# Filler matmuls in more of TensorE's early waits, 256 columns wide instead of 128

## The chip, the cores and the metric

One core of a Trainium2 chip runs the whole kernel. The metric is device time in microseconds, from the start of the program to its end, as the median of the runs of this kernel; the profile shows one execution more closely. The core has a matrix engine (TensorE, PE), a vector engine (VectorE, DVE), an engine for elementwise functions (ScalarE, ACT), a general one (GpSimd, POOL) and queues that issue transfers (among them SyncE, SP). Each works through its own list of instructions in order and waits at semaphores for the others.

## What is computed

A linear attention over 4 batches x 4 heads x 1088 tokens x 32, and behind it a layer with 2048 hidden units. Both are cut here to what matters.

```python
phi(x): a = x @ S1.T; b = x @ S2.T; outer product of a and b per token, 64 values
q_p, k_p = phi(q), phi(k)
kv = einsum('bhsf,bhsd->bhfd', k_p, v);  z = sum(k_p, axis=2)
attn = (q_p @ kv) / (q_p @ z + 1e-6)         # to x: 4352 tokens x 128
h = x @ w_in                                 # 4352 x 2048
out = (h - tanh(h)) @ w_out                  # 4352 x 128
```

## The kernel before

All work is described as operations with a list of what each reads and writes and a cost in nanoseconds. A planner, `_Prog.schedule` (line 139), walks through them once while the program is built. For each engine it keeps the time at which the engine is free, takes the operation that can start first (with keys for ties and for a window of similar starts), and appends it to that engine's list. Costs are written with the operations: `_v(n)` for VectorE, `_a(n)` for ScalarE, `_pe(ns)` for TensorE, and the landing times of the first loads are given by hand. The lists that come out are what the chip runs; waits at semaphores are added by `sync` (line 263). So a planned time decides only the order and, as follows, the fillers.

A filler is a matmul of zeros (tile `zz`, line 434) into a PSUM bank that nothing uses yet, `pso`. When the planner places an operation on TensorE, it looks at the planned wait ahead of it (line 203). If the wait is longer than a limit, `fill` (line 244) puts as many fillers into it as fit. The limit is 60 ns while TensorE becomes free before 7600 ns of the plan (`SOLID`), and `WIDE_GAP` = 1000 ns after. Fillers stop for good when the planner gives out the first bank for output products (`filler[2].used`), which is at o0.0 (line 996). The planned cost of one is 54 ns, doubled while the plan is before 13000 ns (`COLD`). Before `SOLID` a filler may end up to 100 ns after the wait's planned end (`OVER`); after it, it must end 60 ns ahead.

The order of the work in the head, with its lines: the k of batch 0 is transposed on VectorE (L636) and multiplied with the sketches on TensorE (L647, in two parts), brought back by VectorE (L652), and a Gram product of it is taken (L692, two parts), whose small result goes through ScalarE (L698) and one more product (L702). Then the first part of the q sketch (L666, 4 products), then kv (L760, 72 products of v and k's outer products, which VectorE makes at L730). ScalarE copies the result (L373), TensorE transposes it (L777), and the rest of the q sketch follows (L666, 14 products), which ScalarE copies out for VectorE (L678). Then comes the attention's numerator (L866), which gives x, then the layer: h (L981), tanh on ScalarE (L986), and the output products (L996, L1000), which VectorE transposes (L1005) and SyncE writes out. Between these TensorE also transposes w_in (L940) and multiplies it with w_out (L952). ScalarE casts w_in (L934) and copies its transposes (L945). Batches 1 to 3 of the attention follow interleaved with the layer, which runs over groups of 192 to 512 columns (`GCOLS`) and 16 blocks of hidden units each.

Loads are issued at L474 from the queues of SyncE, ScalarE and GpSimd, some of them held until earlier ones have landed.

Of the kernel before, what the change touches and what calls it, by code (L numbers as in the profile page):

```python
# [13 lines left out]
BF16 = mybir.dt.bfloat16  # L14
# [75 lines left out]
class _Prog:  # L90
# [2 lines left out]
    SOLID = 7600.0  # L93
    WARM = 7900.0
    COLD = 13000.0
    WIDE_GAP = 1000.0

    def __init__(self):
        self.ops = []
# [39 lines left out]
    def schedule(self, filler=None):  # L139
# [30 lines left out]
        while n < len(self.ops):  # L170
# [31 lines left out]
            if e == "tensor":  # L202
                if filler is not None and t - free[e] > (60.0 if free[e] < self.SOLID else self.WIDE_GAP) and not filler[2].used:
                    t = max(t, self.fill(filler, free[e], t))
# [39 lines left out]
    def fill(self, filler, a, b):  # L244
        t = a
        while True:
            cold = 2.0 if t < self.COLD else 1.0
            occ = 54.0 * cold
            if t + occ + (60.0 if t > self.SOLID else -self.OVER) > b:
                break  # L250
            o = _Op()
            o.engs = {"tensor": (occ, 215.0)}
            o.fn, o.key, o.dma, o.name, o.mode = filler[0], 0, 0, "fill", "128x128"
            o.deps, o.users, o.vals = {filler[1]: True}, [], []
            o.filler = True
            o.eng, o.t0, o.t1, o.lat = "tensor", t, t + occ, 215.0
            o.inc, o.sem, o.waits, o.known = False, None, [], {}
            o.seq = len(self.order["tensor"])
            self.order["tensor"].append(o)
            t = o.t1  # L260
        return t
# [58 lines left out]
def _v(n):  # L320
    return {"vector": (n / 0.96 + 64.0, 143.0)}
# [22 lines left out]
def bass_polysketch_attn__then__act_tanh_shrink_kernel(  # L344
# [10 lines left out]
    P = _Prog()  # L355
    uid = [0]

    def sb(name, shape, dtype=FP32):
        uid[0] += 1
        return nc.alloc_sbuf_tensor(f"{name}_{uid[0]}", shape, dtype).ap()  # L360

    def ps(name, n=1):
        uid[0] += 1
        return nc.alloc_psum_tensor(f"{name}_{uid[0]}", [128, n * 512], FP32).ap()

    def sbv(name, shape, dtype=FP32):
        return _Val(ap=sb(name, shape, dtype))
# [7 lines left out]
    def slices(pl, parts):  # L375
# [6 lines left out]
    bank_o = _Pool([ps("pso"), psa[:, 1024:1536]], True)  # L382
# [48 lines left out]
    wiT = [sbv("wiT", [128, 8, 128], BF16) for _ in range(2)]  # L431
    wch = sbv("wch", [128, DM], BF16)
    wcl = sbv("wcl", [128, DM], BF16)
    zz = sbv("zz", [128, 256], BF16)

    zop = P.add(_v(128), lambda e, n: e.memset(zz.ap[:, :], 0.0), w=[zz], key=-99000)  # L436
    filler = (lambda e, n: e.matmul(bank_o.slots[0][0][:, 0:128], zz.ap[:, 0:128], zz.ap[:, 128:256],  # L437
                                    start=True, stop=True), zop, bank_o)

    def pool_op(fn, r=(), w=(), n=100, key=-50000.0):  # L440
        return P.add(_g(n), fn, r=r, w=w, key=key)
# [4 lines left out]
        fill=1.0, base=0, channel_multiplier=1), r=[ident], w=[ident])  # L446
# [10 lines left out]
    for pl, f, val in ((kT_p, lambda a: a[:, 1088:1152], 0.0),   # L457
                       (m_p, lambda a: a[:, :, 8:9], 1e-6)):
        for i, s_ in enumerate(pl.slots):
            o = pool_op(lambda e, n, a=f(s_[0]), val=val: e.memset(a, val), n=64, key=-49000)  # L460
# [83 lines left out]
    t = T_FIRST  # L544
# [478 lines left out]
    for name in ORDER.split():  # L1023
        b = int(name[1])
# [85 lines left out]
```

## Time and profile before

| what | us |
|---|---|
| median of 5 runs (lowest, highest) | 109.80 (109.14, 110.00) |
| the profiled execution's own time | 109.84 |
| its span, from the first to the last instruction | 107.8 |
| busy: PE, ACT, DVE, POOL | 99.7, 83.4, 67.2, 5.0 |
| fillers (L437): 48 products, busy | 5.0 |
| mean granted TensorE clock | 0.968 of full |

The fillers run in three groups, 36 from 1.06 us, 8 from 5.77 and 4 from 6.71. The program has 3434 recorded instructions, of which 1462 are matmuls and as many weight loads.

How to read it: times of the timeline are counted from the first instruction. The page gives the busy share of each engine in 40 slices of 2.7 us, in tenths (9 is 90% or more), and the granted TensorE clock in tenths of full speed. A matmul's duration includes the time that its last column takes to leave the array, which overlaps with the next matmul, so counts times durations are not sums. In a list of stretches the columns are start and end, length, and for each engine its busy time and number of instructions, then the granted clock, the share of the DMA engines and GB/s. In a timeline they are start, duration, engine, line, operation, what it writes and reads, and in brackets the engine's idle time before it and what ended that. A chain is followed back from the last instruction to whatever released it at each step.

### The profile page before, as it was taken

What the parts mean: (1) busy time and instruction counts of PE and PEld (TensorE: products, weight loads), DVE (VectorE), ACT (ScalarE), POOL (GpSimd) and SP (SyncE); (2) the same over time, 40 slices, a digit from 0 to 9 for tenths busy, and PEclk for the clock granted to TensorE, in tenths of its full rate; (3) what the DMA queues carried; (4) which work ended last, traced back from release to release, by engine and by line L of the source; (5) the groups of instructions that cost most, each with busy time, mean ns of one, the idle gap of its engine ahead of it and who ended that gap; (6) DMA issues with size and microseconds to landing.
All of it is one profiled execution on the core that took longest, in us unless ns stands there. A gap on an engine that the chain in (4) does not pass through costs nothing.

```text
span 107.8 us, 3434 instructions
## 1 busy us (share of the span) xinstructions
PE 99.7 (92%) x1462; PEld 53.3 (49%) x1462; DVE 67.2 (62%) x114; ACT 83.4 (77%) x174; POOL 5.0 (5%) x23
## 2 busy tenths in 40 slices
PE   6974899899999999999999999999999999999960
PEld 6834788475664446543346443444433443344730
DVE  4679834998992999999999990899620020020210
ACT  0400368999648888878898987999989999999950
POOL 5600420000000000000000000000000000000000
PEclk9996559999999999999999999999999999999999
DMA  2999899776039736006930150033003315004153
GB/s 65 227 247 218 245 125 271 269 186 207 14 41 277 204 88 138 6 6 124 275 106 0 20 84 0 6 50 47 0 0 45 59 19 78 0 15 68 17 76 58
DMA packets 26431, 10.73 MB, mean 100 GB/s; under 512 B 21153, under 2 KB 24241, under 8 KB 26417
## 3 DMA queue, kind: packets, MB, share of 16 engines
q1 hardware_dynamic: 22368, 8.69, 35.0%
q0 software_dynamic: 2112, 0.54, 5.1%
q10 hardware_dynamic: 1936, 1.29, 5.0%
q8 instruction: 11, 0.18, 0.7%
q14 instruction: 4, 0.02, 0.1%
HBM read 8.81 MB, written 2.23 MB: 102 GB/s over the span
## 4 chain that ended last, share of the span: by engine, by line
PE 40%; ACT 32%; DVE 13%; DMA 9%; issue 2%; SPq 1%; DVEq 0%
ACT th L986 27%; PE pso L996 11%; PE psh L981 9%; DMA vL<-in_v_dram 7%; PE psa L866 6%; PE psa L760 3%; DMA sq<-in_S_dram 3%; ACT xT L373 3%; DVE w L730 2%; DVE abc L807 2%; DVE qp L850 2%; DVE ot L1005 1%; PE pso L1000 1%; PE psh L666 1%; PE psa L799 1%
## 5 line engine op out<-in xcount | busy, mean ns | idle before, releaser
L986 ACT ACTIVATE th<-psh 128x512 bf16<-128x512 f32 (+4 forms) x114 | 63.3, 656 | 3.0 <-PE psh L981 2.8
L981 PE MATMUL psh<-xT,wi 128*128 128x512 bf16 (+4 forms) x142 | 44.0, 348 | 0.4 <-ACT th L986 0.4
L996 PE MATMUL pso<-th,wo 128*128 128x512 bf16 (+3 forms) x128 | 40.4, 358 | 0.3 <-DVE ot L1005 0.2
L996 PEld LDWEIGHTS pso<-th,wo 128*128 128x128 bf16 x128 | 11.7, 97 | 16.4 <-ACT th L986 4.5
L981 PEld LDWEIGHTS psh<-xT,wi 128*128 128x128 bf16 x142 | 13.4, 98 | 12.1 <-ACT th L986 1.6
L1005 DVE STREAM_TRANSPOSE ot<-pso 128x512 f32<-128x512 f32 (+3 forms) x8 | 5.2, 645 | 15.7 <-PE pso L996 15.7
L855 DVE STREAM_TRANSPOSE qpT<-qp 128x768 f32<-128x768 f32 (+1 forms) x14 | 12.1, 861 | 0.4
L730 DVE TENSOR_TENSOR w<-abk 128x768 f32<-128x768 f32 (+2 forms) x12 | 11.0, 943 | 0.1
L850 DVE TENSOR_TENSOR qp<-ap,abc 128x768 f32<-128x768 f32 (+1 forms) x13 | 10.7, 826 | 0.1
L986 ACT ACTIVATE th<-psa 128x1024 bf16<-128x1024 f32 (+2 forms) x10 | 8.6, 907 | 0.0
L866 PE MATMUL psa<-qpT,kvb 32*32 32x128 f32 (+4 forms) x336 | 8.2, 309 | 0.1
L866 PE MATMUL psh<-qpT,kvb 32*32 32x128 f32 (+4 forms) x112 | 8.2, 310 | 0.0
L996 PE MATMUL psa<-th,wo 128*128 128x512 bf16 (+1 forms) x32 | 7.4, 314 | 0.3 <-ACT th L986 0.2
L866 PEld LDWEIGHTS psa<-qpT,kvb 32*32 32x32 f32 x336 | 5.0, 103 | 3.1 <-DVE qpT L855 1.2
L1005 DVE STREAM_TRANSPOSE ot<-psa 128x512 f32<-128x512 f32 (+1 forms) x2 | 1.1, 550 | 8.6 <-PE psa L996 8.6
L437 PE MATMUL pso<-zz 128*128 128x128 bf16 x48 | 5.0, 290 | 1.1 <-DVE zz L436 1.1
L610 DVE STREAM_TRANSPOSE qT<-qL 128x576 f32<-128x576 f32 (+3 forms) x8 | 5.4, 708 | 0.4 <-DMA qL<-in_q_dram 0.4
L981 PE MATMUL psa<-xT,wi 128*128 128x512 bf16 (+1 forms) x18 | 5.6, 349 | 0.0
L437 PEld LDWEIGHTS pso<-zz 128*128 128x128 bf16 x48 | 4.4, 137 | 1.5 <-DVE zz L436 1.1
L804 DVE STREAM_TRANSPOSE abc<-psh 128x288 f32<-128x288 f32 x3 | 1.4, 483 | 5.1 <-PE psh L799 5.0
L698 ACT ACT_TABLE_LOAD x1 | 1.3, 1283 | 4.2 <-issue 4.2
L373 ACT CAST xT<-psa 128x64 bf16<-128x64 f32 (+4 forms) x11 | 4.4, 457 | 0.0
(87 smaller groups left out, 99.5 us busy)
## 6 DMA issues: line engine op xcount, KB each, us to landing
vL<-in_v_dram SPq DMA_DIRECT2D x11, 144.0 KB, 3.8
wif<-in_moe_w_in_dram SPq DMA_DIRECT2D x4, 256.0 KB, 6.3
out_dram<-ot SPq DMA_DIRECT2D x16, 64.0 KB, 2.0
kL<-in_k_dram SPq DMA_DIRECT2D x3, 288.0 KB, 3.1
qL<-in_q_dram SPq DMA_DIRECT2D x3, 288.0 KB, 3.3
kL<-in_k_dram SPq DMA_DIRECT2D x3, 256.0 KB, 3.0
qL<-in_q_dram SPq DMA_DIRECT2D x3, 256.0 KB, 3.9
wo<-in_moe_w_out_dram POOLq DMA_DIRECT2D x2, 256.0 KB, 5.9
```

What stands on the lines that cost most here:

```text
L373: return e.copy(o, i) if name == "scalar" else e.tensor_copy(o, i)
L437: filler = (lambda e, n: e.matmul(bank_o.slots[0][0][:, 0:128], zz.ap[:, 0:128], zz.ap[:, 128:256], start=True, stop=True), zop, bank_o)
L610: P.add(_v((z - a) * 32), lambda e, n: e.transpose(qTs[b][:, a * 32:z * 32], val.ap), r=[val], w=tvs, key=nk(), name=f"qT{b}.{i}")
L730: P.add(_v(nx * 64), lambda e, n: e.tensor_tensor(out=wv.ap[:, 0:nx * 64].rearrange("p (x i j) -> p x i j", i=8, j=8), in0=abh(0)[:, :, :, ...
L760: i = e.matmul(bk[2].ap[h * 32:(h + 1) * 32, 0:64], vL[b][:, h, blk * 32:(blk + 1) * 32], wvs[b, p].ap[:, (bi * 4 + h) * 64:(bi * 4 + h + ...
L850: P.add(_v(cn * 256), lambda e, n, qp=qp, c0=c0, cn=cn: e.tensor_tensor(out=qp.ap[:, 0:cn * 256].rearrange("p (x i j) -> p x i j", i=8, j= ...
L855: P.add(_v(cn * 256), lambda e, n, qp=qp, o0=o0, cn=cn: e.transpose(qt.ap[:, o0 * 256:(o0 + cn) * 256], qp.ap[:, 0:cn * 256]), r=[qp], w=[ ...
L866: i = e.matmul(banks[g].ap[h * 32:(h + 1) * 32, 0:nb * 32], kvb.ap[g * 32:(g + 1) * 32, x, h * 32:(h + 1) * 32], qq[g * 32:(g + 1) * 32, 0 ...
L981: return e.matmul(hv.bank(j // per)[:, c:c + n_], wib[:, jb * 128:(jb + 1) * 128], xt, start=True, stop=True)
L986: return e.activation(out=th.ap[:, 0:m * n_].rearrange("p (j x) -> p j x", x=n_), in_=i, func=AF.Tanh, scale=-1.0)
L996: fn = lambda e, n, x=x, st=st, sp_=sp_: e.matmul(ov.ap[:, 0:n_], wob[:, x, :], ths[x][0].ap[:, ths[x][1]:ths[x][1] + n_], start=st, stop=sp_)
L1005: P.add(_vp(n_), lambda e, n: e.transpose(ot.ap[:, 0:n_], ov.ap[:, 0:n_]), r=[ov], w=[ot], key=-60000, name=f"ot{gi}")
```

## The change

The limit for waits that begin after 7600 ns falls from 1000 to 150 ns. `fill` tries a filler of 256 columns first and takes one of 128 when the wide one does not fit; a wide one may not end after the wait's planned end, even before `SOLID`. The tile of zeros grows by 128 columns, with the planned cost of its memset.

```diff
-    WIDE_GAP = 1000.0
+    WIDE_GAP = 150.0
...
             cold = 2.0 if t < self.COLD else 1.0
-            occ = 54.0 * cold
-            if t + occ + (60.0 if t > self.SOLID else -self.OVER) > b:
-                break
+            margin = 60.0 if t > self.SOLID else -self.OVER
+            w = 1
+            occ = 107.0 * cold
+            if t + occ + max(margin, 0.0) > b:
+                w = 0
+                occ = 54.0 * cold
+                if t + occ + margin > b:
+                    break
             o = _Op()
             o.engs = {"tensor": (occ, 215.0)}
-            o.fn, o.key, o.dma, o.name, o.mode = filler[0], 0, 0, "fill", "128x128"
+            o.fn, o.key, o.dma, o.name, o.mode = filler[0][w], 0, 0, "fill", "128x128"
...
-    zz = sbv("zz", [128, 256], BF16)
-
-    zop = P.add(_v(128), lambda e, n: e.memset(zz.ap[:, :], 0.0), w=[zz], key=-99000)
-    filler = (lambda e, n: e.matmul(bank_o.slots[0][0][:, 0:128], zz.ap[:, 0:128], zz.ap[:, 128:256],
-                                    start=True, stop=True), zop, bank_o)
+    zz = sbv("zz", [128, 384], BF16)
+
+    zop = P.add(_v(192), lambda e, n: e.memset(zz.ap[:, :], 0.0), w=[zz], key=-99000)
+    filler = ([lambda e, n, w=w: e.matmul(bank_o.slots[0][0][:, 0:w], zz.ap[:, 0:128], zz.ap[:, 128:128 + w],
+                                          start=True, stop=True) for w in (128, 256)], zop, bank_o)
```

## The prediction

> **What bounds the kernel now.** I read the page's slices first, to see whether TensorE's clock ever falls.
>
> ```profile
> PE   6974899899999999999999999999999999999960
> ACT  0400368999648888878898987999989999999950
> PEclk9996559999999999999999999999999999999999
> ```
>
> A slice is 2.7 us. From 20 us to the end TensorE and ScalarE are both nearly full and the clock is whole, so that stretch will move only as a block. The one irregular place is the head: slices 5 to 7 (10.8 to 18.9 us) have a clock of 0.5 to 0.6. Second view: stretches of 3.41 us, laid so that they begin and end where the granted clock changes.
>
> ```profile
> core 0: us, PE busy (x), PEclk, DMA share, GB/s
> 5.71:9.12 3.41, 2.07 (x54) 1.00 0.99 233
> 9.12:12.53 3.41, 2.23 (x41) 0.50 0.97 238
> 12.53:15.95 3.42, 3.42 (x68) 0.50 0.97 153
> 15.95:19.36 3.41, 3.33 (x90) 1.00 1.44 287
> 101.27:104.68 3.41, 2.85 (x28) 1.00 0.31 45
> ```
>
> The clock is full up to 9.12, half from 9.12 to 15.95, full again after: 6.83 us, two of these stretches. Each follows the one before it: busy 2.07 of 3.41 (61%) and then half clock; 65% and still half; 100% and then full; 98% and 84% and still full. (The first fillers too ran slowly: 36 in 4.02 us, one every 0.107 us; those after 5.7 us 0.056 apart.) Third view: TensorE's timeline, with the waits in the brackets.
>
> ```profile
> 7.24 0.51 PE L647 MATMUL psh<-kT,wab 64*32 64x160 f32 x16
> 8.84 0.31 PE L692 MATMUL psa<-abk 128*32 128x32 f32 x10 [1.09 <-DVE abk L652]
> 9.42 0.29 PE L702 MATMUL psa<-gm,s2r 128*32 128x8 f32 x8 [0.28 <-ACT gm L698]
> 10.10 1.17 PE L666 MATMUL psa<-wq,qT 128*128 128x96 f32 x4 [0.38 <-DVE wq L715]
> 11.79 2.15 PE L760 MATMUL psa<-w,vL 128*32 128x64 f32 x72 [0.52 <-DMA vL<-in_v_dram]
> ...
> 19.64 0.39 PE L981 MATMUL psh<-xT,wi 128*128 128x256 bf16 x2 [0.36 <-ACT th L986]
> ```
>
> Last view: the chain that ended last, in order of time.
>
> ```profile
> 4.40 7.35 DMA vL<-in_v_dram
> 11.79 2.15 PE psa L760 x72
> 13.94 0.54 PE psh L940 x4
> 14.48 0.64 PE psa L777 x2
> 15.12 1.33 PE psh L666 x8
> 16.48 0.48 ACT abc L678
> ```
>
> Up to 11.75 us the end hangs on v's landing. Nothing that TensorE does earlier matters, and the half clock before 11.79 is free. From 11.79 to 16.48 the chain lies on TensorE at half clock: that is the price to be won or not.
>
> **The change, step by step.** Sum against the profiled execution: 109.84 us, of which 107.82 is span and 2.02 lies around it; the median of the runs shown is 109.80, so I take it as the same.
>
> *Where fillers go.* The limit WIDE_GAP applies to planned waits that begin after 7600 ns of the plan. The plan follows from the costs in the code; before, it has waits there of 858 ns (ahead of the second gram product), 467 (ahead of L702), 507 (ahead of the first L666), 118, 201 (ahead of L777) and 542 (ahead of h0.4, the 19.64 row). All are under 1000, so none was filled; five are over 150. A wide filler is planned at 214 ns (107 after 13000), a narrow one at 108 (54), with a margin of 60. So: 858 takes 3 wide and 1 narrow, 467 takes 1 and 1, 507 takes 2, 201 takes one narrow, 542 takes 4 and 1. In all 10 wide and 4 narrow.
>
> *The early fillers.* Of 48 narrow ones (36, 8, 4), the same arithmetic makes 18 wide and 1 narrow, 3 and 2, 1 and 2: 27 instructions and 49 units of 128 columns in place of 48. Records: 41 instead of 48, each with its weight load. The columns are the same, so the clock should still rise at 5.71. The first wait ends one unit later than before: the fillers ended at about 4.87, the next work started at 5.16, so 0.11 fits. The plan behind it moves by some 70 ns; the matmul order could then differ in a place, which I can't exclude and cost at nothing.
>
> *The larger memset.* VectorE's 0.17 us for 128 words becomes about 0.25; its next memsets end at 2.2 and it idles 0.52 until 2.72. Hidden, save that fillers start 0.07 later.
>
> *What the fillers cost in place.* TensorE runs in order, so the instruction behind a filler waits for it. A wide one counts as two units (the 256-wide L981 at 18.56 are 0.109 apart, four in 0.61). In the 1.09 wait: at 0.056 a unit, 7 units are 0.39, at half clock 0.75: room either way. Ahead of L702: 3 units, 0.17 or 0.32, against 0.28 shown (the product before is issued by about 8.95, its end holds a drain of 0.2): 0 to 0.05 late. Ahead of L666: 4 units, 0.22 or 0.43, against 0.38 and a similar drain: 0 to 0.1. Both lie before v's landing, which leaves 0.52. Ahead of L777: one unit, 0.06 or 0.11, beside ScalarE's copy (14.01 to 14.38) which L777 waits for: 0 to 0.1. Ahead of h0.4: 9 units at full clock, 0.50, against 0.36 plus the drain: 0 to 0.15; behind it ScalarE's tanh is queued after a copy at 19.96, so h0.4 has some 0.4 to spare. No row shows a change between filler and 32-column products with a wait this short; 0 to 0.1 each. I take 0.2 in all, ends 0 and 0.5.
>
> *What they do to the clock.* This is the whole question, and no row shows it; I bound it. Fillers raise the busy share of 5.71 to 9.12: the 1.09 wait gets 0.39 of streaming and about 0.17 of drain, 0.56; with the 0.28 wait's beginning 2.65 of 3.41, 78%. 61% let the clock fall, 84% kept it: 78 is nearer the upper. If it falls nevertheless, 9.12 to 12.53 gets both waits, 2.23 + 0.28 + 0.38 = 2.89, 85%: 65% did not raise it, 100% did, so it stands in the middle. If it stays, the same stretch runs at full clock and needs less time: 2.4 to 2.5 busy, about 72%, so it might fall at 12.53 instead.
>
> *A rule against it.* The Trainium skill (TensorE: Matmul & The Clock Gate, "Why this matters for your kernels") says that only pauses beyond about 3 us between bursts bring the half clock back. The row: the longest pause here is 1.09 us and the clock fell. By the rule waits of 0.3 to 1.1 us never mattered and the fillers give 0; by the row a thinly used stretch is enough, and filling is worth up to 1.3. The measurement decides. The same page (Part 1) has a window of 3.41 us that runs free of the kernel's start, which agrees with the 6.83 us here. If so, each execution has its own boundaries, and the median mixes the cases below.
>
> *What a full clock is worth.* With it from 11.79: the 72 products take 1.19 instead of 2.15 (the same 72 of a later batch, L745 at 41.84): 0.96. The two L777 products take 0.48 from start to next work, half of that gone: 0.24. Five of the first eight L666 products at 0.11 instead of 0.21: 0.45 (their starts before and after 15.95). TensorE: 1.65. ScalarE between 14.01 and 18.99 idles only 0.82, but it starts 0.96 earlier, so it follows: about 1.5 at the first tanh. The weights do not stop it: the first half of wo lands at 16.9, used at 19.87. If the clock returns only at 12.53, 28 of the 72 stay slow: 0.57 + 0.24 + 0.45, about 1.2. Less the 0.2 of fillers: 1.3 and 1.0. From there to the end work is in order and full, k and q of the next batch have landed before VectorE takes them, so the shift should reach the end. What is late next is ScalarE's own row of copies and tanh.
>
> **The rivals.**
> 1. Clock falls at 9.12, back at 12.53: 109.84 - 1.0 = 108.8. Chance 0.27.
> 2. Clock never falls: 109.84 - 1.3 = 108.5. Chance 0.26. For both: 78% and 85% against the rows.
> 3. Clock holds at 9.12, falls at 12.53, returns at 15.95: 52 of the 72 run fast (-0.65), L777 stays slow, and of the L666 products eight instead of five do (+0.3): -0.35, 109.5. Chance 0.15. For it: fillers are sized for half clock and cover only half a wait at full clock.
> 4. Not what it says: the fillers (zeros, 14 of them) don't tip any stretch, cost 0 to 0.2: 109.9. Chance 0.15.
> 5. Slower: the half clock is not removed but moved behind v's landing. In the old place 2.67 of its 6.83 us (9.12 to 11.79) cost nothing. If it begins at 12.53 and lasts two stretches, to 19.36, then all 14 L666 products are slow (nine more at +0.10, 0.9), and so are L866 and the transposes and first h products from 17.04 to 19.28 (2.2 us at full clock; half beside ScalarE, so 1.1 of it counts). Against the 0.65 won on the products: 0.9 + 1.1 - 0.65 = +1.35, about 111.2. It decides when 12.53 to 15.95 is not busy enough to raise the clock: it was 100%, and with fast products in front a wait for v's copy opens in it. Chance 0.17.
>
> **How the numbers follow.** The likeliest is case 1, 108.8. The range runs from 108.3 (case 2 and 0.2 less filler cost) to 110.2 (case 4 with its cost); outside lie case 5 and a tail. A measurement can tell about 0.5% (0.55 us) from no change. Faster by more: cases 1 and 2 and a third of 3: 0.58. Within: the rest of 3, and 4: 0.25. Slower: 0.17. Own range of the faster cases: 108.3 to 109.2.
>
> **What would show it.** L437 x41, 32 wide and 9 narrow; fillers in the waits ahead of L692, L702, L666, L777 and the third pair of L981. Granted clock of 9.12 to 12.53 and of 12.53 to 15.95: 1.00 in case 2, 0.50 and 1.00 in case 1. L760's 72 at 1.2 to 1.6 instead of 2.15; the copy L678 at 15.0 to 15.3 instead of 16.48; the first tanh near 17.7 instead of 18.99. I am wrong if the clock rows are as before, if v lands later, or if the head is earlier and the tanh after 20 us is not.

## The result and the profile after

| | before | after |
|---|---|---|
| median, us (executions) | 109.76 (79) | 108.74 (44) |
| the profiled execution: own time, span | 109.84, 107.8 | 108.84, 106.7 |
| mean granted clock of it | 0.968 | 0.996 |

The ratio is 0.9964, 95% interval 0.9945 to 0.9982: faster by 0.4%, where 0.9% was forecast. The median lies at the forecast 108.8. The two disagree because every ratio here leaves out each execution more than 1.5% above its own kernel's fastest among those timed together, which keeps 23 of 79 before (median 109.07) and 34 of 44 after (108.60). A ratio of this size is also near what one program against itself gave (0.9965, at the end of the experiments), so it alone doesn't show a gain; the medians and the granted clock do. Which groups of executions lie behind the two medians is the main finding below.

First the page's clock row of after, to hold against that of before, and the row of the fillers (count, busy time, mean ns).

```profile
PE   5997899899999999999999999999999999999960
PEclk9999999999999999999999999999999999999998
...
L442 PE MATMUL pso<-zz 128*128 128x256 bf16 (+1 forms) x41 | 7.9, 352 | 1.1 <-DVE zz L441 1.1
```

The hole in the clock is gone. Next, stretches of 3.41 us that begin where the clock first changed in this execution (6.97), with busy time, clock and DMA as before.

```profile
core 0: us, PE busy (x), PEclk, DMA share, GB/s
6.97:10.39 3.42, 2.50 (x53) 1.00 1.07 250
10.39:13.80 3.41, 2.94 (x88) 1.00 0.80 251
13.80:17.21 3.41, 3.36 (x93) 1.00 1.26 187
```

Here a stretch that was busy for 73% was followed by full clock; before, one of 61% was followed by half. The share alone does not decide it, as the repeats below show. Then TensorE's timeline.

```profile
5.79 1.44 PE L442 MATMUL pso<-zz 128*128 128x256 bf16 x7
7.45 0.51 PE L652 MATMUL psh<-kT,wab 64*32 64x160 f32 x16 [0.21 <-DVE kT L641]
7.88 0.27 PE L697 MATMUL psa<-abk 128*32 128x32 f32 x8
8.09 0.61 PE L442 MATMUL pso<-zz 128*128 128x256 bf16 x4
9.40 0.31 PE L697 MATMUL psa<-abk 128*32 128x32 f32 x10 [0.70 <-DVE abk L657]
...
10.66 0.69 PE L671 MATMUL psa<-wq,qT 128*128 128x96 f32 x4
11.73 1.21 PE L765 MATMUL psa<-w,vL 128*32 128x64 f32 x72 [0.38 <-DMA vL<-in_v_dram]
12.89 0.40 PE L945 MATMUL psh<-identb,wi 128*128 128x128 bf16 x4
13.12 0.27 PE L442 MATMUL pso<-zz 128*128 128x256 bf16 x1
13.44 0.44 PE L782 MATMUL psa<-ident,kvd 128*128 128x128 f32 x2
13.71 1.70 PE L671 MATMUL psh<-wq,qT 128*128 128x96 f32 x14
```

(Lines past 245 have moved by five.) The 72 products take 1.21 instead of 2.15, and the last L671 group starts 1.20 earlier, although the work in front of v's landing is later: the second Gram product (L697) at 9.40 instead of 8.84. The planner has put the second L652 ahead of the first L697. v hides that.

ScalarE's timeline shows how far the gain reaches. Before, then after: the first tanh and a later group of three.

```profile
18.99 1.08 ACT L986 ACTIVATE th<-psh 128x512 bf16<-128x512 f32 x2
...
25.63 1.39 ACT L986 ACTIVATE th<-psh 128x384 bf16<-128x384 f32 x3
```

```profile
17.29 1.08 ACT L991 ACTIVATE th<-psh 128x512 bf16<-128x512 f32 x2
...
24.56 1.33 ACT L991 ACTIVATE th<-psh 128x384 bf16<-128x384 f32 x3
```

1.70 us earlier at the first, 1.07 at the second, 1.07 at the end (span 107.8 to 106.7). So 0.6 us of the head's gain is lost between 17 and 25 us. It shows in the second of these lines of TensorE's timeline of after, inside the second run of numerator products:

```profile
20.61 0.24 PE L871 MATMUL psa<-qpT,kvb 32*32 32x96 f32 x1
21.28 0.27 PE L871 MATMUL psa<-qpT,kvb 32*32 32x96 f32 x2 [0.42 <-issue]
```

"issue" means that it waited for nothing that the profile shows. From the product before (20.61) to this one (21.28) 0.67 us pass. ScalarE then waits for the result, the copy to x. Its copy in after, and in the kernel `full_rate` below, which has the same order here, the same first tanh (17.28) and no such pause:

```profile
21.68 0.24 ACT L378 CAST xT<-psh 128x96 bf16<-128x96 f32 x1 [0.38 <-PE psh L871]
```

```profile
21.10 0.34 ACT L378 CAST xT<-psh 128x96 bf16<-128x96 f32 x1
```

So the pause costs 0.58, nearly all of the 0.6. (This numerator starts only 1.37 earlier than before, 19.95 against 21.32. But three more products of the layer stand ahead of it than before, and three fewer behind it, so that part is not lost.)

### The profile page after: what moved, and what is told of

The parts are those of the page before. It is cut to its first block, busy times and chain, and to the rows that moved or that the text cites. A ratio compares the mean times of both kernels' runs of the same rounds, so it can differ in the third digit from the quotient of the medians.

```text
span 106.7 us, 3421 instructions
## 1 busy us (share of the span) xinstructions
PE 99.5 (93%) x1455; PEld 51.3 (48%) x1455; DVE 67.4 (63%) x114; ACT 83.5 (78%) x174; POOL 5.0 (5%) x23
## 4 chain that ended last, share of the span: by engine, by line
PE 42%; ACT 31%; DMA 17%; DVE 4%; SPq 1%; issue 1%
ACT th L991 27%; PE pso L1001 12%; DMA vL<-in_v_dram 11%; PE psh L986 10%; PE psa L871 6%; DMA qL<-in_q_dram 3%; ACT xT L378 3%; DMA sq<-in_S_dram 3%; PE psa L765 2%; PE psa L750 2%; SPq L479 1%; PE psh L671 1%; PE pso L1005 1%; PE psh L871 1%; PE psa L782 1%
## 5 line engine op out<-in xcount | busy, mean ns | idle before, releaser
L986 PE MATMUL psh<-xT,wi 128*128 128x512 bf16 (+4 forms) x142 | 44.0, 347 | 0.1
L986 PEld LDWEIGHTS psh<-xT,wi 128*128 128x128 bf16 x142 | 13.4, 98 | 11.5 <-ACT th L991 1.1
L442 PE MATMUL pso<-zz 128*128 128x256 bf16 (+1 forms) x41 | 7.9, 352 | 1.1 <-DVE zz L441 1.1
L986 PE MATMUL psa<-xT,wi 128*128 128x512 bf16 (+1 forms) x18 | 5.6, 349 | 0.0
L1001 PEld LDWEIGHTS psa<-th,wo 128*128 128x128 bf16 x32 | 2.6, 97 | 3.6 <-ACT th L991 3.1
```

The source lines that it names most:

```text
L442: filler = ([lambda e, n, w=w: e.matmul(bank_o.slots[0][0][:, 0:w], zz.ap[:, 0:128], zz.ap[:, 128:128 + w], start=True, stop=True) for w i ...
L986: return e.matmul(hv.bank(j // per)[:, c:c + n_], wib[:, jb * 128:(jb + 1) * 128], xt, start=True, stop=True)
L1001: fn = lambda e, n, x=x, st=st, sp_=sp_: e.matmul(ov.ap[:, 0:n_], wob[:, x, :], ths[x][0].ap[:, ths[x][1]:ths[x][1] + n_], start=st, stop=sp_)
```

## The experiments

**Theories.** *Clock*: what decides an execution is how much half clock it has and where; fillers matter through the columns they stream. *Records*: fewer instructions are what helps. *Order*: fillers delay what stands behind them. *Given back*: a gain in the head is lost later, at instruction fetch or at a transfer.

**The changed kernel again**, unchanged.

> The changed kernel once more, unchanged. Clock theory: what decides an execution is where the half-clock stretch lies; with the fillers most executions have none after 11.7 us and end near 108.5, and those with a mean granted clock under 0.985 end above 109.7; median 108.7, before 109.8. Rival (an early gain is lost again later): the head is 1.7 us earlier in the profile but the end only 1.1, so the profile again shows some 0.6 us given back between 20 and 27 us, either at a pause in L871 that waits for nothing shown or at the landing of the second half of q of batch 1.

Measured: median 108.83 (22), before 109.93, ratio 0.9913 (0.9878 to 0.9947). The pause was there again, with nearly the same length:

```profile
20.85 0.27 PE L871 MATMUL psa<-qpT,kvb 32*32 32x96 f32 x2 [0.39 <-issue]
```

Its clock held too, though the first stretch with full clock was less busy than in after, 67%:

```profile
5.60:9.01 3.41, 2.30 (x54) 1.00 0.97 255
```

With the mean granted clock of each execution the groups are plain. One half-clock stretch of 3.41 us takes 0.016 off the mean, and up to 0.01 is lost behind the last products (in after, from 105.96 us on). So a mean of 0.975 to 0.985 stands for one stretch in the head, less for two (or, in a few, more), more for none. The 79 executions of before in the table above have no clock on record; those timed beside the experiments, and `before_c`, have.

| half-clock stretches | before: executions, median | after and its repeat |
|---|---|---|
| two | 99, 110.30 | none |
| one | 98, 109.27 | 15, 110.07 |
| none | 7, 110.32 | 51, 108.61 |

The kernel before behaves like two kernels, half and half, and its median (109.76) stands where the two groups overlap: those with two stretches begin at 109.58, those with one reach past 110. The execution that I predicted from had two stretches. The changed kernel has none in 51 of 66.

The seven in the last row do not fit at first sight: four of them took over 110.3. The mean counts the time ahead of the first record of the clock as full. In the profile of `both` (below; mean 0.992) the first record stands at 13.85, and the kv products ahead of it ran slowly:

```profile
12.77 1.70 PE L765 MATMUL psa<-w,vL 128*32 128x64 f32 x72
```

A clock that rises late may thus be what the four had; no profile of them shows it.

**Parts of the change.** Narrow fillers in the same waits (`WIDE_GAP = 150` in the kernel before), and wide ones without the new waits (`WIDE_GAP = 1000` in the changed one):

> The kernel before with the limit at 150 and narrow fillers alone: about the same columns of zeros as after, in 71 instructions instead of 41. Clock theory: only the columns matter, so as the changed kernel, 108.7 (within 0.2), full clock from 7 us on. Rival (records): the larger number of instructions costs, 109.0 to 109.5, with pauses in TensorE that wait for nothing shown.

> The changed kernel with the limit back at 1000: fillers 256 wide only where the kernel before had narrow ones, 26 instructions instead of 48. Clock theory: as before, 109.7 to 109.9, half clock at some time between 9 and 16 us in most executions. Rival (records): fewer instructions alone bring a part of the gain, 109.2 to 109.4.

Measured: narrow in all waits 109.11, ratio 0.9960 (0.9925 to 0.9995); wide in the old waits 109.73, 0.9994 (0.9954 to 1.0034), with half clock in all 14. So the width alone brings nothing (*records* falls) and the new waits bring the gain. But the narrow fillers missed what I expected of them (108.7 within 0.2): 10 of 22 executions had a half-clock stretch. Those without stood at 108.47, so it was not the number of instructions that cost. Whether the width counts for the clock (15 of 66 with it) stays open; the columns are nearly the same.

```diff
-    WIDE_GAP = 150.0
+    WIDE_GAP = 600.0
```

> The changed kernel with the limit at 600: of the five new groups only the one in the longest wait (858 ns planned) is left. Clock theory: that group adds 0.11 to the busy share of the stretch up to about 9 us but nothing to the next, so the half clock is seen in more executions than with all five (15 of 66) and fewer than with none (all but 3 of 110): about half, median 109.1 to 109.4. Rival (the other four groups do nothing for the clock and cost time): as the changed kernel or better, 108.5 to 108.7.

Measured: 108.92, ratio 0.9915 (0.9881 to 0.9949), half clock in 8 of 22. The limit had left two groups, not one: the profile has three fillers ahead of L671 too (at 9.79). Two of five groups thus keep most of the gain; the rival (that the others cost time) got no support: 108.57 without half clock, as after.

**More filling.** Fillers counted at the full-clock rate (`COLD = 5600`), and four wide ones in the wait for v, which the planner does not see:

```diff
-                         mode="128x32", name=f"kvmm{b}.{p}", after=[P.scmm])
+                         mode="128x32", name=f"kvmm{b}.{p}", after=[P.scmm, P.vf])
...
         q_tok(b, 0, 2, abc, bk[1:2])
+        P.vf = P.add(_pe(1.0), lambda e, n: [filler[0][1](e, n) for _ in range(4)][-1], r=[zz],
+                     key=-50000.0 + seq[0] + 0.5, mode="128x128", name="vf", after=[P.ops[-2]])
```

> The changed kernel with fillers counted at the full-clock rate from 5600 ns of the plan on, so that each wait holds about twice the columns (58 instructions). Clock theory: the busy share of the stretches from 7 to 12 us rises, so fewer executions fall to half clock: median 108.4 to 108.6 and hardly any above 109.5. Rival (order): where the clock is half the fillers overrun L702, L666 and L777 by 0.2 to 0.4 us each, so the median is 108.9 to 109.3.

> The changed kernel with four more wide fillers between the first q sketch and the kv products, the wait for v's landing that the planner does not see. Clock theory: the stretch that holds 9 to 12 us is busier by 0.13, so fewer executions have a half-clock stretch: 0 to 2 of some 22 with a mean clock under 0.985 (the changed kernel had 15 of 66), and the median falls from 108.75 to about 108.6. Rival (order): where v lands early the fillers delay the kv products by up to 0.4 us, so that the median is 108.8 to 109.0.

Measured: 108.92, ratio 0.9917 (0.9886 to 0.9948), and 108.63, ratio 0.9924 (0.9896 to 0.9952). Neither had a half-clock execution in 22, so *clock* is right about the cause: fillers in more waits, none of half clock. Nor was much won. With v's wait filled the profile shows v landed at 10.85 and the products starting at 11.53, behind the four fillers: there *order* is right about a price. At the full rate the executions stood at 108.92, those of the changed kernel timed with them and without half clock at 108.72; the profile has no filler in the way of v (the products start at 11.78, after a wait of 0.50 for it), so a price there is not shown.

v's wait filled also says something of the first measure: its stretch from 5.84, 68% busy, was followed by full clock too.

```profile
5.84:9.26 3.42, 2.31 (x55) 1.00 1.00 267
```

**The pause.** Three profiles (after, its repeat, narrow fillers alone) pause at record 705 of TensorE's list (weight loads, products and semaphore waits counted from 0), though in the third another instruction stands there, and after pauses at 449 too, 256 earlier. A fetch of 16 KB of instructions had ended 1.41 to 1.58 us before each pause did; if it holds the 256 records between the pauses, they are 64 bytes each. The next kernel moves the list by 34 records:

```diff
-            if t + occ + max(margin, 0.0) > b:
+            if t < 5100.0 or t + occ + max(margin, 0.0) > b:
```

> The changed kernel with its first group of fillers (planned before 5.1 us) narrow again: the same columns, 58 fillers instead of 41, so that every later instruction of TensorE stands 34 records further back. Fetch theory: TensorE paused at record 705 of its list in three profiles (after, the same again, narrow fillers alone), whatever instruction stood there, about 1.45 us after the last packet of the second fetch of its instructions; with the list moved by 34 the fetch is asked for earlier in the work, the pause in the second numerator product is gone as in the kernel counted at full rate, and from v's landing to the end it takes 94.7 us in the profile instead of 95.0. Median among executions without half clock 108.3 to 108.4, in place of 108.6 to 108.7. Rival (the wait there is for data): the pause is at the same product as in the changed kernel, and the times are its own.

Measured: at 705 the profile has 0.18 us left (20.86 to 21.04) of the 0.67, and 108.22 without half clock, near what the fetch theory said, but half clock in 10 of 22, so the median was 109.23 (ratio 0.9907, 0.9870 to 0.9944). It also puts the order of L697 and L652 back, so it moved more than the list. The profiled execution had its stretch late:

```profile
core 0: us, PE busy (x), PEclk, DMA share, GB/s
7.47:10.88 3.41, 2.33 (x30) 1.00 1.04 248
10.88:14.29 3.41, 2.95 (x79) 0.50 0.72 192
```

68% busy, and the clock fell. That is the share at which it stayed with v's wait filled, and more than in the repeat (67%). So the busy share of one stretch, as the profile counts it, doesn't decide; what does is open.

> The changed kernel with a narrow first group and two wide fillers in the wait for v (instead of four). Fetch and clock theory together: no pause at record 705, so 108.2 without half clock, and fewer executions with it than the narrow first group alone (10 of 22): 0 to 4, median 108.2 to 108.4. Rival (a narrow first group is itself what lets the clock fall): again near half of the executions, median above 108.8.

Measured, with a narrow first group and two wide fillers in v's wait: no pause at 705, 108.34 without half clock, but half clock in 8 of 22; median 108.97, ratio 0.9967 (0.9927 to 1.0008). The rival is right here. With a narrow first group 28 of 66 executions fell, with the changed kernel's 15 of 66. Why is open.

**v's landing.** q's second part from SyncE's queue, to stand behind v:

```diff
-    load_q(next(lk), 0, 1, "scalar")
+    load_q(next(lk), 0, 1, "sync")
```

> The changed kernel with the load of the second part of q of batch 0 (416 KB) issued from SyncE's queue behind v's parts instead of from ScalarE's. Theory (the end hangs on v's landing: in six profiles the end came 94.7 to 96.3 us after it, with v at 10.9 to 11.75): v lands about 1.5 us earlier, at 10.0 to 10.5, and the end follows by 0.8 to 1.2: 107.6 to 107.9. Rival (the weights or q are next): q's second part lands at 11.8 or later and w_in as before, ScalarE and VectorE then wait for these, and less than 0.3 is won: 108.5.

> The last two of these that change the order: q's second part behind v, and the first group of fillers narrow. If the two gains are separate: 107.3 to 107.6. If q or the weights are next: as the kernel with q moved alone.

Measured: 111.35, ratio 1.0111 (1.0034 to 1.0189), and 111.34, 1.0171 (1.0111 to 1.0231). My edit did not do what it was meant to: without a wait for the first load, q was issued at 1.47, ahead of the rest of k and of v, and the kv products started at 13.82 and 12.77. It tests nothing of the theory except how dear a late k is. Mended with `[s1]` as a further argument:

> As the try with q's second part on SyncE's queue, but with the same wait for the first load that the others have, so that it really stands behind v (in that try it was issued first, at 1.47 us, and pushed k and v back). Theory (the end hangs on v's landing): v lands at 10.0 to 10.5 instead of 10.9 to 11.7 and the end follows by 0.8 to 1.2: median 107.6 to 108.0 where no half clock falls in. Rival (q is next): q's second part lands after 11.7, VectorE's transpose of it and the second q sketch wait, and at most 0.3 is won: 108.3 to 108.6.

> The last two together. If v's landing bounds the head and the pause is gone: 107.2 to 107.6. If q is next: as without it, 108.2 to 108.4.

Measured: 108.17, ratio 0.9877 (0.9827 to 0.9926), and 108.03, 0.9883 (0.9818 to 0.9948), less won than I expected of either. In the first, v landed at 9.45, 2.2 us earlier than in the profile of after, but the end came only 0.9 earlier. TensorE's timeline of the first:

```profile
7.96 0.61 PE L442 MATMUL pso<-zz 128*128 128x256 bf16 x4
9.27 0.31 PE L697 MATMUL psa<-abk 128*32 128x32 f32 x10 [0.70 <-DVE abk L657]
...
10.54 0.69 PE L671 MATMUL psa<-wq,qT 128*128 128x96 f32 x4
11.15 1.04 PE L765 MATMUL psa<-w,vL 128*32 128x64 f32 x60
```

No wait stands in front of L765 any more: the Gram product, the fillers and the first q products are the bound. So the theory is right that v was the bound, not how far. And the next bound is not q, as the rival had it: VectorE takes q's second part at 11.00 without a wait.

> The kernel with q's second part behind v once more. If v's landing bounds the head: 108.0 to 108.3 as in the first six executions, 0.4 to 0.6 under the changed kernel (108.75), with few or no half-clock executions. If those six were luck: 108.6 to 108.8.

> The kernel with a narrow first group, two fillers in the wait for v, and q's second part behind v, once more: 107.9 to 108.2, if the pause at record 705 and v's landing are separate costs at or below the kernel with q moved alone; if the narrow first group lets the clock fall again, a third of the executions above 109.3 and a median of 108.5 or more.

Measured: 108.44, ratio 0.9885 (0.9826 to 0.9944), and 108.18, ratio 0.9825 (0.9755 to 0.9896). In the 12 executions of each none had half clock; medians of the 12 are 108.30 and 108.04. So the second, with narrow first group, two fillers in v's wait and q behind v, has the lowest median here, some 0.6 below the changed kernel without half clock (108.61), though the two were not timed together.

**Where the half clock lies.** Three more profiles of the kernel before:

> The kernel before, one look for its clock. Reading to be tested: an execution with a mean clock of 0.979 to 0.984 (one half-clock stretch) has it so that most of it lies ahead of v's landing (begin between 7.5 and 9.5 us, end by 12 to 13), and from v's landing to the end it takes 95.0 to 95.6 us instead of the 96.1 of the two-stretch profile. Rival: the single stretch lies behind 11 us, and the time from v to the end is 95.9 or more, as in the narrow-first kernel.

> The kernel before, a second look; the same expectation as the first. Should both show the two-stretch clock (0.968), they tell nothing new but the spread of v's landing: the end 96.0 to 96.3 us after it.

> The kernel before, with timed rounds. Reading to be tested, as for the two looks: in an execution with a mean clock of 0.979 to 0.984 the single half-clock stretch begins between 7.5 and 9.5 us and ends by 13, and from v's landing to the end it takes 95.0 to 95.6 us. Rival: it lies behind 11 us and the end comes 95.9 us or more after v's landing; then the place of the stretch does not explain why one costs less here than in the changed kernel.

Measured: all three had two stretches. The first two were late; the first of them:

```profile
core 0: us, PE busy (x), PEclk, DMA share, GB/s
10.62:14.03 3.41, 2.39 (x76) 0.50 0.86 250
14.03:17.44 3.41, 3.41 (x19) 0.50 1.46 145
```

| kernel | half clock, us | v landed | end after v |
|---|---|---|---|
| before; before_c | 9.12 to 15.95; 8.71 to 15.54 | 11.75; 11.33 | 96.1; 96.1 |
| before_a; before_b | 10.62 to 17.44; 10.97 to 17.80 | 11.62; 11.88 | 96.8; 96.9 |
| narrow first group | 10.88 to 14.29 | 11.30 | 96.0 |
| after; its repeat; full rate | none | 11.69; 11.33; 11.74 | 95.1; 95.0; 94.7 |

The same 6.83 us come with 0.7 to 0.8 more behind v when they begin 1.5 to 2.3 us later: 0.9 to 1.0 us of them lie in front of v's landing, not 2.6. A single stretch of the kernel before was never profiled, so that it lies earlier than the changed kernel's single ones (not profiled either) is only argued from this, not shown. The third was also timed: the same program against itself gave 0.9965 (0.9932 to 0.9999). A ratio of this size is thus near what two measurements of one kernel can differ by here.

## Why the prediction was wrong

**The step that failed** is the base of the sum: "the median of the runs shown is 109.80, so I take it as the same". The profiled execution had two half-clock stretches, and its time is near the median only because the median falls between the middles of two groups, 110.30 and 109.27. A gain of 1.0 is right against the profiled execution (109.84 to 108.84) and against the mixture (109.76 to 108.74). Against the executions with one stretch it is 109.27 to 108.61, 0.7. The ratio compares still less: it keeps of before only what is under 109.32, where later no execution with two stretches lay (their least is 109.58), so 109.07 to 108.60. I had written that each execution has its own boundaries, and then reckoned from one.

That the median came out at 108.74 where I said 108.8 is partly luck: the case that I put there, a clock back at 12.53, is not what the profile shows, and two errors in the sum, told below, had opposite signs.

**The clock**: right that it could hold, as in 51 of 66. Case 2 (0.26) came true, not the likeliest, case 1. But the busy share, by which I weighed the cases, is too coarse a measure: stretches of 67 and 68% were followed by full clock, and another of 68% by half.

**What a full clock is worth**: 1.5 expected at the first tanh, 1.70 measured; L765 took 1.21 against 1.19.

**"The shift should reach the end"**: failed, 1.70 became 1.07. I looked at landings of q and k, which were not the bound, and not at the pause in TensorE's own list (0.58). That failure and the underrated start (1.3 taken) cancelled in part.

**Rival 5**, half clock moved behind v's landing, two stretches, 111.2: no execution of the changed kernel had two. One stretch is left in 15 of 66, at 110.07, 0.8 more than one of before. That fits a place further back, but no profile caught one; the single stretch of the narrow first group lay mostly behind v's landing (10.88 to 14.29; 11.30).

**Fillers**: 41 as reckoned, but 36 wide and 5 narrow, not 32 and 9, since the planner changed the order of L697 and L652. I put that at nothing; the second Gram product came 0.56 later, which v's landing hid, and this work became the bound once v came earlier. The 0.2 for delays was not seen: the third pair of L986 starts 1.70 earlier (17.94 against 19.64), like the tanh before it.

**The rule against it** fell: the clock was lost with no pause over 1.1 us, in before (the longest 1.09) and with the narrow first group (0.60 ahead of the fall). The gain by the fillers in short waits says the same.

## What to carry over

Before reckoning from one profile, ask whether its time is typical or a member of a group: look at the spread of the times and at the clock of each execution. To judge half clock, ask what it lies in front of: here the part ahead of v's landing, which bounds the head, cost little. And when a head gets faster, check what else feeds the engine, its instruction list too.

## What was not expected of the hardware

TensorE's list seems to come in blocks of 256 instructions: the pauses of after stand at records 449 and 705. A block could be used only 1.4 to 1.6 us after its last packet, some 2.4 us after the fetch began. In after the second fetch began at 18.88 and the pause ended at 21.28, 2.40 later; the small rest of a pause with the narrow first group ended 2.44 after its fetch. A burst of small products (128 records in under 1 us) outran it. In before the fetch began at 19.27 and record 705 came up at 21.91, 2.64 later, so nothing paused. Fewer records in front put the boundary later in the work: saving records cost 0.58 us in the profile of after, and some 0.3 to 0.4 by the medians without half clock (108.61 against 108.22 and 108.34, not timed together).
